# Loading the last 768 columns of one block of output weights as row groups of 63, 54 and 11 partitions

## The chip, the cores and the metric

One core of a Trainium2 chip runs the whole kernel. The metric is the device time of one launch in microseconds (us), as the median of several runs. "Span" is the stretch from the first to the last instruction in one execution that was taken with the hardware profiler. The core has 16 DMA engines, which move data from device memory to the on-chip memory of 128 partitions. The compute engines are PE (matrix), DVE (vector), ACT (scalar) and POOL; SP issues nearly all of the transfers.

## The reference

One token (a row of 1024 numbers) goes through two branches, which a gate mixes:

```python
g = sigmoid((x * gate_w).sum(-1))
a = attention(x)      # 32 query heads, 4 key/value heads, cache of 65536 positions, head size 128
b = mixer(x)          # gelu(x @ w_in), split, layernorm of one half, product, @ w_out
return g * a + (1 - g) * b

# attention
q = x @ wq                                   # 1024 x 4096
p = softmax(q @ k_cache.T * Dh ** -0.5)      # 8 query heads share one key/value head
return (p @ v_cache).reshape(4096) @ wo      # wo: 4096 x 1024
```

All tensors are bf16. The key and value caches are 64 MiB each, `wq` and `wo` 8 MiB each, `w_in` 7 MiB and `w_out` 3.5 MiB: some 162 MB are read once for a result of 2 KB.

## The kernel before, in words

**The stream of loads.** All large inputs pass through one ring in on-chip memory (the region `RING` of the tensor `arena`). The list `stream` fixes their order when the program is built; `load` appends to it and `issue` (L377 to L392) turns entries into transfers on SP's queue. An entry goes out as soon as every ring grain of 1024 columns that it overwrites has been marked as used by `done`. So SP waits for the compute engines and then issues transfers well ahead of the data. Each entry is one transfer of 128 rows, one per partition, and the 16 DMA engines take eight rows each. The order is: `wq`; the keys and values of the four heads in 16 blocks, with `w_in` and `w_out` among the first; then `wo`.

**The output weights.** `rows(A_wo, i, 8)` is quarter i of `wo`: 1024 of its rows, eight to a partition, so one partition receives 8192 numbers (16384 contiguous bytes). Quarters 0, 1 and 2 are one entry each. Quarter 3 is cut by `WO_CUT` into pieces of 5, 2 and 1 of the eight rows, that is 10240, 4096 and 2048 bytes per partition. These six entries end the stream. Just ahead of the very last one `issue` puts a store of the (still zero) output row; the store of the result follows at the end of the program.

**The work on them.** `wo_rows(0)`, `wo_rows(1)`, `wo_piece(2)` and three calls of `wo_piece(3, ...)` multiply the attention output with the six pieces on PE. `spin(n)` puts n matrix products of no use between them. A cast on DVE (L775) and the store (L366) end the kernel.

**Waits.** `Recorder.op` notes each operation with what it reads and writes; `plan` derives the semaphore waits and `emit` writes the instructions. A transfer adds 16 to the semaphore of its ring grain when it is complete, and `op` counts that in `dma_count`; a reader waits for the counted total.

**Small loads.** Four small transfers go out on ACT's queue at the start: `A_x` and `gate_w` as eight rows of 256 bytes each, `B_w_sp` and `B_b_sp` as two bytes each.

Of the kernel before, what the change touches and what calls it, by code (L numbers as in the profile page):

```python
# [17 lines left out]
class Recorder:  # L18
# [9 lines left out]
        self.ahead = 0  # L28
        self.early = 0

    def op(self, eng, fn, r=(), w=(), dma=None):
        o = Op()
        o.eng, o.fn, o.inc, o.count = eng, fn, False, 0
        o.dma = None
        deps = {}
        for k in r:
            if k in self.writer:
                deps[id(self.writer[k])] = (self.writer[k], True)
        for k in w:
            if k in self.writer:  # L40
                deps.setdefault(id(self.writer[k]), (self.writer[k], False))
            for x in self.readers.get(k, ()):
                deps.setdefault(id(x), (x, False))
        o.deps = list(deps.values())
        for k in r:
            self.readers.setdefault(k, []).append(o)
        for k in w:
            self.writer[k] = o
            self.readers[k] = []
        if dma is not None:  # L50
            self.dma_count[dma] = self.dma_count.get(dma, 0) + 16
            o.dma = (dma, self.dma_count[dma])
        o.idx = len(self.ops)
        self.ops.append(o)
        return o
# [40 lines left out]
    def emit(self, nc):  # L96
        waits = self.plan()
        sems = {e: nc.alloc_semaphore("eng_" + e) for e in self.ENGINES}
        dsem = {k: nc.alloc_semaphore("dma_%s" % k) for k in self.dma_count}
        final = {k: v for k, v in self.dma_count.items()}  # L100

        def run(eng, handle):
            for o, ws in zip(self.ops, waits):
                if o.eng != eng:
                    continue
                for d in ws:
                    if d.dma:
                        handle.wait_ge(dsem[d.dma[0]], d.dma[1])
                    else:
                        handle.wait_ge(sems[d.eng], d.count)  # L110
                last = o.fn(handle)
                if o.dma:
                    last.then_inc(dsem[o.dma[0]], 16)
                elif o.inc:
                    last.then_inc(sems[eng], 1)

        body = nc.cur_bb.bb
        gate = next(i for i, x in enumerate(body.instructions)
                    if isinstance(x, mybir.InstDrain) and x.engine == mybir.EngineType.SP)
        first = len(body.instructions)  # L120
        run("SP", nc.sync)
        nc.sync.wait_ge(dsem["out"], final["out"])
        made = list(body.instructions)
        moved = made[first:first + self.ahead]
        assert all(isinstance(x, mybir.InstDMACopy) for x in moved)
        body.instructions = made[:gate] + moved + made[gate:first] + made[first + self.ahead:]
        run("POOL", nc.gpsimd)
        run("PE", nc.tensor)
        first = len(body.instructions)
        run("ACT", nc.scalar)  # L130
        made = list(body.instructions)
        gate = next(i for i, x in enumerate(made) if isinstance(x, mybir.InstDrain) and x.engine == mybir.EngineType.Activation)
        moved = made[first:first + self.early]
        assert all(isinstance(x, mybir.InstDMACopy) for x in moved)
        body.instructions = made[:gate] + moved + made[gate:first] + made[first + self.early:]
        run("DVE", nc.vector)


def bass_gated_mix__gqa_block_cached__mixer_gmlp__decode_kernel(
# [45 lines left out]
    OFF = {}  # L185
# [16 lines left out]
    arena = nc.alloc_sbuf_tensor("arena", [128, NA], BF16)  # L202
# [52 lines left out]
    P = R.op  # L255
# [46 lines left out]
    stream = []  # L302
# [1 line left out]

    GRAN = 1024

    def load(keys, src, off):

        n = len(stream)
        w = src.shape[1]  # L310
        for i, key in enumerate(keys):
            place[key] = (n, off + i * (w // len(keys)), w // len(keys))
        stream.append((keys, off, src))

    def rows(w, i, c):

        return w[128 * c * i:128 * c * (i + 1), :].rearrange("(p c) n -> p (c n)", c=c)
# [12 lines left out]
    def load_k(n, slot):  # L330
        load([("k", n)], kv(A_k_cache, n), slot * SUB)

    def load_k2(n, slot):
        load([("k", n), ("k", n + 1)], kv(A_k_cache, n, True), slot * SUB)

    def load_v2(n, off):
        load([("v", n), ("v", n + 1)], kv(A_v_cache, n, True), off)
# [18 lines left out]
    WO_AT = [0, 8 * DO, 16 * DO, 24 * DO]  # L356
    WO_CUT = [(0, 5), (5, 7), (7, 8)]
    for i in range(3):
        load([("wo", i, 0)], rows(A_wo, i, 8), WO_AT[i])
    for c0, c1 in WO_CUT:  # L360
        load([("wo", 3, c0)], rows(A_wo, 3, 8)[:, DO * c0:DO * c1], WO_AT[3] + DO * c0)

# [2 lines left out]
    def store():  # L365
        P("SP", lambda e: e.dma_start(out[0, 0].rearrange("(q n) -> q n", n=QW), osrc), r=["orow"],  # L366
          w=["out"], dma="out")
# [5 lines left out]
    def grains(off, w):  # L373
        return list(range(off // GRAN, (off + w + GRAN - 1) // GRAN))

    def issue():

        while issued[0] < len(stream):
            n = issued[0]
            keys, off, src = stream[n]  # L380
            w = src.shape[1]
            gr = grains(off, w)
            if any(k not in used for x in gr if x in owner for k in owner[x]):
                return
            for j, x in enumerate(gr):
                owner[x] = (keys[j * len(keys) // len(gr)],)
            if n == len(stream) - 1:
                store()
            P("SP", lambda e, o=OFF["RING"] + off, w=w, src=src: e.dma_start(arena[:, o:o + w], src),
              w=[("slot", x) for x in gr], dma="s%d" % gr[0])  # L390
            issued[0] += 1

    def use(key):
        n, off, w = place[key]
        assert n < issued[0], key
        return arena[:, OFF["RING"] + off:OFF["RING"] + off + w], [("slot", x) for x in grains(off, w)]

    def done(key):
        used.add(key)
        issue()  # L400

    issue()


# [8 lines left out]
      r=["m32"], w=["sel"])  # L413
    P("DVE", lambda e: e.tensor_reduce(mq, vw(idf, 0, [[1, 16], [16, 8]]), AXX, ALU.add), r=["idf"], w=["mq"])
    P("DVE", lambda e: e.tensor_reduce(mhalf, vw(idf, 0, [[32, 2], [64, 2], [1, 32]]), mybir.AxisListType.XY, ALU.add),
      r=["idf"], w=["mhalf"])
# [4 lines left out]
    for fe in range(4):  # L421
        P("POOL", lambda e, fe=fe: e.tensor_copy(vw(sele, 128 * fe, [[32, 4], [1, 32]]),
                                                vw(idb, 64 * (fe // 2) + fe % 2, [[0, 4], [2, 32]])),
          r=["idb"], w=[KSE])
# [5 lines left out]
    def f(e):  # L430
# [7 lines left out]
      r=["oneb", "wsp", "bsp"], w=["mb"])  # L438
# [6 lines left out]
      r=["ones", "gs"], w=[KTB])  # L445
# [4 lines left out]
      r=["g"], w=["omg"])  # L450
# [3 lines left out]
    wqs, keys = use(("wq", 0))  # L454
# [354 lines left out]
```

## Time and profile before

| | |
|---|---|
| median of 9 runs | 381.87 us (381.76 to 382.10) |
| the profiled execution's own time | 381.87 us |
| its span | 380.6 us |
| bytes read | 162.01 MB, 426 GB/s over the span |
| share of the 16 DMA engines' time taken by SP's queue | 98.8% |
| busy: PE, DVE, ACT, POOL | 61%, 54%, 6%, 2% |
| granted clock of PE, mean | 0.848 |

How to read it: the shares of busy time are of the span. The queue named q1 is that of SP, q10 that of ACT; q8 and q14 carry instructions. A "packet" is what one DMA engine moves at a time: here one row of a transfer, or the four bytes with which an engine reports that it is done with its share of one. 1.27 us of the profiled execution's time lie outside the span.

### The profile page before, as it was taken

The page shows a single profiled execution, that of the slowest core. Times are in us where ns is not written, and L with a number is a line of the kernel's source. Part 1 is how long each engine was busy: PE and PEld are TensorE (multiplying, and loading weights), DVE is VectorE, ACT ScalarE, POOL GpSimd, SP SyncE. Part 2 cuts the span into 40 slices and gives each one's busy share as a digit, 9 for nine tenths or more (in the row PEclk, how much of TensorE's full clock was granted, in tenths as well). Part 3 has the DMA queues.
Part 4 walks back from the last instruction along what each step waited for, and adds up shares of the span by engine and source line. Part 5 has one row for each costly group of instructions (what it writes and reads, how often), then busy time and mean ns, then how long its engine had stood idle before and what let it go on. Part 6 is the DMA issues. An engine that isn't in the chain of part 4 may idle for free.

```text
span 380.6 us, 2581 instructions
## 1 busy us (share of the span) xinstructions
PE 232.7 (61%) x1449; PEld 57.8 (15%) x836; DVE 204.4 (54%) x162; ACT 23.2 (6%) x24; POOL 8.4 (2%) x37
## 2 busy tenths in 40 slices
PE   0060488466648924894787328952995983639386
PEld 0010011011101200121111001220111110212024
DVE  4011596678389525965892248745874872412020
ACT  1000000010420000002100000022000000220010
POOL 5000000000000000000000000000000000000000
PEclk9997599798959975999698958985898796959789
DMA  9998989999989999999999999999999999999996
GB/s 441 420 434 372 482 381 443 437 493 424 415 386 441 441 429 434 441 427 413 470 441 441 441 434 427 408 420 441 434 420 425 444 441 441 429 410 437 406 428 251
DMA packets 4254, 162.17 MB, mean 426 GB/s; under 512 B 532, under 2 KB 532, under 8 KB 788
## 3 DMA queue, kind: packets, MB, share of 16 engines
q1 hardware_dynamic: 4208, 162.01, 98.8%
q8 instruction: 9, 0.15, 0.2%
q10 hardware_dynamic: 36, 0.00, 0.0%
q14 instruction: 1, 0.01, 0.0%
HBM read 162.01 MB, written 0.00 MB: 426 GB/s over the span
## 4 chain that ended last, share of the span: by engine, by line
DMA 57%; DVE 21%; PE 20%; ACT 1%; issue 1%; ACTq 0%; SPq 0%; DVEq 0%
DMA arena<-in_A_k_cache_dram 34%; DVE arena L502 17%; DMA arena<-in_A_v_cache_dram 10%; DMA arena<-in_A_wo_dram 8%; PE scp L260 6%; PE scp L262 5%; DMA arena<-in_B_b_sp_dram 5%; PE obt L260 4%; PE obt L262 3%; DVE arena L539 2%; PE fbt L712 1%; ACT arena L534 1%; ACTq L288 0%; PE fbt L660 0%; ACT arena L656 0%
## 5 line engine op out<-in xcount | busy, mean ns | idle before, releaser
L502 DVE STREAM_TRANSPOSE arena<-arena 128x2048 f32<-128x2048 f32 x64 | 142.8, 2282 | 45.8 <-DMA arena<-in_A_k_cache_dram 31.5
L260 PE MATMUL scp<-arena 128*128 128x512 bf16 (+1 forms) x275 | 111.4, 421 | 85.5 <-DVE arena L502 85.0
L262 PE MATMUL scp<-arena 128*128 128x512 bf16 (+1 forms) x279 | 111.0, 416 | 0.0
L260 PE MATMUL obt<-arena 128*64 128x512 bf16 (+2 forms) x334 | 63.1, 418 | 21.0 <-DMA arena<-in_A_v_cache_dram 21.0
L262 PE MATMUL obt<-arena 128*64 128x512 bf16 (+2 forms) x334 | 62.3, 413 | 0.0
L260 PEld LDWEIGHTS scp<-arena 128*128 128x128 bf16 (+1 forms) x275 | 27.4, 103 | 196.2 <-issue 99.9
L539 DVE STREAM_TRANSPOSE arena<-arena 128x2048 bf16<-128x2048 bf16 x7 | 16.2, 2311 | 31.3 <-PE obt L262 29.1
L260 PEld LDWEIGHTS obt<-arena 128*64 128x64 bf16 (+1 forms) x334 | 18.5, 113 | 74.5 <-issue 57.2
L534 ACT ACTIVATE arena<-arena 128x2048 bf16<-128x2048 f32 x8 | 16.0, 2002 | 218.0 <-DVE arena L531 194.9
L519 DVE TENSOR_SCALAR_CACHE_REDUCE arena<-scp 128x2048 f32<-128x2048 f32 x8 | 18.3, 2292 | 16.0 <-PE scp L262 16.0
L580 PE MATMUL mbt<-arena 128*128 128x128 bf16 x16 | 2.0, 264 | 12.6 <-DVE arena L575 12.6
L542 DVE STREAM_TRANSPOSE arena<-arena 128x1024 bf16<-128x1024 bf16 x2 | 2.5, 1245 | 12.5 <-PE obt L262 12.5
L568 DVE RECIPROCAL arena<-mbt 128x1 f32<-128x1 f32 x4 | 0.6, 139 | 15.8 <-PE mbt L563 15.8
L490 POOL COPY arena<-arena 32x32 bf16<-32x32 bf16 x16 | 3.2, 203 | 235.2 <-PE scp L262 211.2
L531 DVE TENSOR_REDUCE arena<-mbt 128x1 f32<-128x32 f32 x4 | 0.8, 191 | 13.8 <-PE mbt L528 13.8
L437 PE MATMUL mbt<-arena 1*128 1x2 bf16 x1 | 0.2, 158 | 12.3 <-DMA arena<-in_B_b_sp_dram 12.3
L439 DVE COPY arena<-mbt 128x2 f32<-128x2 f32 x1 | 0.2, 159 | 12.2 <-PE mbt L437 12.2
L432 PE MATMUL scp<-arena 8*128 8x1 bf16 x8 | 0.6, 196 | 8.7 <-DVE arena L427 8.7
L775 DVE CAST arena<-fbt 36x128 bf16<-36x128 f32 x1 | 0.3, 282 | 10.1 <-PE fbt L712 10.1
L712 PE MATMUL fbt<-arena 128*32 128x128 bf16 x128 | 4.1, 220 | 1.4 <-DMA arena<-in_A_wo_dram 1.4
L712 PEld LDWEIGHTS fbt<-arena 128*32 128x32 bf16 x128 | 3.6, 97 | 3.0 <-DMA arena<-in_A_wo_dram 1.8
L624 ACT ACTIVATE arena<-arena 128x28 f32<-128x28 f32 x1 | 0.2, 227 | 57.8 <-DVE arena L623 57.8
(91 smaller groups left out, 54.8 us busy)
## 6 DMA issues: line engine op xcount, KB each, us to landing
arena<-in_A_k_cache_dram SPq DMA_DIRECT2D x6, 4096.0 KB, 33.2
arena<-in_A_v_cache_dram SPq DMA_DIRECT2D x2, 4096.0 KB, 26.8
arena<-in_B_w_in_dram SPq DMA_DIRECT2D x1, 7168.0 KB, 31.5
arena<-in_A_wo_dram SPq DMA_DIRECT2D x3, 2048.0 KB, 34.2
arena<-in_B_w_out_dram SPq DMA_DIRECT2D x1, 3584.0 KB, 22.1
arena<-in_A_wo_dram SPq DMA_DIRECT2D x1, 1280.0 KB, 31.1
arena<-in_A_wo_dram SPq DMA_DIRECT2D x1, 512.0 KB, 31.8
arena<-in_A_wo_dram SPq DMA_DIRECT2D x1, 256.0 KB, 31.6
```

The source lines that it names most:

```text
L260: return e.matmul(*a, **kw)
L262: one = e.matmul(*a, **kw).ins
L432: ins = e.matmul(tb[:, c:c + 1], vw(xm, c, [[8, 128]], 0, 8), oneb[0:8, 0:1], start=(c == 0), stop=(c == KC - 1), skip_group_check=True)
L490: P("POOL", lambda e, pb=pb: e.tensor_copy(vw(qpad, 24 + 32 * pb, [[QP, 4], [1, 8]], 32 * pb, 32), vw(qall, 8 * g, [[32, 4], [1, 8]], 32 * ...
L502: P("DVE", lambda e: e.transpose(ktb(i).bitcast(F32), sl[:, 4096 * p:4096 * (p + 1)].bitcast(F32)), r=keys[4 * p:4 * p + 4], w=[("kt", i % ...
L519: P("DVE", lambda e: e.tensor_scalar(scs(j), scp[:, :], 0.0, None, op0=ALU.add, op1=ALU.max, accum_out=maxc[:, j:j + 1]), w=[("sc", j % 2) ...
L531: P("DVE", lambda e: e.tensor_reduce(gcol(g, K_NB), mb[:, 0:32], AXX, ALU.min), w=[("nb", g), "mb"])
L534: P("ACT", lambda e: e.activation(psb2, scs(j), ACTF.Exp, bias=gcol(j // 2, K_NB), scale=SCALE, accum_out=lp[:, j:j + 1]), r=[("sc", j % 2 ...
L539: P("DVE", lambda e: e.transpose(ptsb2, psb2), r=["psb"], w=[("ptsb", 0), ("ptsb", 1)])
L542: P("DVE", lambda e: e.transpose(ptsb(n), ab("PSB", 1024, 1024 * (n % 2))), r=["psb"], w=[("ptsb", n % 2)])
L580: ins = e.matmul(mb[:, 0:128], sel[:, 128 * c:128 * (c + 1)], osc[:, 128 * c:128 * (c + 1)], start=(c == 0), stop=(c == 3))
L712: ins = e.matmul(fb[32 * b:32 * (b + 1), 0:QW], ovz[:, z:z + 32], sl[:, o:o + QW], start=False, stop=(i == 3 and c == 7), tile_position=(0 ...
```

## The change

The entry of quarter 0 of `wo` is split into four transfers, which SP issues one after the other. The first carries all 128 partitions without their last 768 columns (14848 of 16384 bytes per partition). The other three carry these 768 columns (1536 bytes per partition) for the partitions 0 to 62, 63 to 116 and 117 to 127. The source of each is viewed as `(i j) n -> i j n` with i = 3, 9 and 11, so that its rows fall to 3, 9 and 11 DMA engines, with 21, 6 and 1 rows for each. All four report to one semaphore, and the count that a reader waits for is 64 in place of 16. The loaded bytes and their places are the same.

```diff
-    def op(self, eng, fn, r=(), w=(), dma=None):
+    def op(self, eng, fn, r=(), w=(), dma=None, parts=1):
...
-            self.dma_count[dma] = self.dma_count.get(dma, 0) + 16
+            self.dma_count[dma] = self.dma_count.get(dma, 0) + 16 * parts
...
                 if o.dma:
-                    last.then_inc(dsem[o.dma[0]], 16)
+                    for x in last if isinstance(last, list) else [last]:
+                        x.then_inc(dsem[o.dma[0]], 16)
...
-    def load(keys, src, off):
+    def load(keys, src, off, cut=None):
...
-        stream.append((keys, off, src))
+        dst = arena[:, OFF["RING"] + off:OFF["RING"] + off + w]
+        parts = [(dst, src)]
+        if cut:
+            c, heights = cut
+            parts = [(dst[:, 0:w - c], src[:, 0:w - c])]
+            p = 0
+            for k, h in heights:
+                parts.append((dst[p:p + h, w - c:w], src[p:p + h, w - c:w].rearrange("(i j) n -> i j n", i=k)))
+                p += h
+            assert p == 128
+        stream.append((keys, off, w, parts))
...
-        load([("wo", i, 0)], rows(A_wo, i, 8), WO_AT[i])
+        load([("wo", i, 0)], rows(A_wo, i, 8), WO_AT[i], cut=(768, ((3, 63), (9, 54), (11, 11))) if i == 0 else None)
...
-            P("SP", lambda e, o=OFF["RING"] + off, w=w, src=src: e.dma_start(arena[:, o:o + w], src),
-              w=[("slot", x) for x in gr], dma="s%d" % gr[0])
+            P("SP", lambda e, todo=todo: [e.dma_start(dst, x) for dst, x in todo],
+              w=[("slot", x) for x in gr], dma="s%d" % gr[0], parts=len(todo))
```

More of the change, by code (lines that the diff above doesn't have):

```diff
@@ L379, in issue @@
             n = issued[0]
-            keys, off, src = stream[n]
-            w = src.shape[1]
+            keys, off, w, todo = stream[n]
             gr = grains(off, w)
```

## The prediction

> **What bounds the kernel now.** I read the page's slices and queues first, then the chain that ended last, then the end of the stream in stretches of 0.2 us, and last the single packets of the trace.
>
> The page, slices and queues:
>
> ```profile
> DMA  9998989999989999999999999999999999999996
> GB/s 441 420 434 372 482 381 443 437 493 424 415 386 441 441 429 434 441 427 413 470 441 441 441 434 427 408 420 441 434 420 425 444 441 441 429 410 437 406 428 251
> q1 hardware_dynamic: 4208, 162.01, 98.8%
> q8 instruction: 9, 0.15, 0.2%
> ```
>
> SP's queue takes 98.8% of all DMA engine time, so the stream of loads is the bound. PE (61%) and DVE (54%) have room. The last slice alone is thin. Nine packets of instructions travel on the same engines.
>
> The chain of waits in its last 36 us (start, length, what):
>
> ```profile
> 345.51 31.10 DMA arena<-in_A_wo_dram
> 376.60 0.14 issue
> 376.74 1.75 PE fbt L712 x56
> 378.49 0.01 issue
> 378.50 0.42 PE fbt L712 x8
> ```
>
> PE waits for the first piece of quarter 3 until 376.60, multiplies two pieces (1.75 us), and at 378.50 starts on the third; in the timeline PE's weight loads idle 0.19 us for that third transfer. So data and PE arrive together, and both follow the stream's end.
>
> The end of the stream, windows (the last two columns are the DMA share and GB/s):
>
> ```profile
> 375.80:376.00 0.20, 0.20 (x3) 0.00 (x0) 0.00 (x0) 0.00 (x0) 0.00 (x0) 1.00 0.91 358
> 376.40:376.60 0.20, 0.00 (x0) 0.00 (x0) 0.00 (x0) 0.00 (x0) 0.00 (x0) 1.00 0.54 216
> 377.40:377.60 0.20, 0.20 (x16) 0.20 (x11) 0.00 (x0) 0.00 (x0) 0.00 (x0) 1.00 0.53 205
> 377.60:377.80 0.20, 0.20 (x15) 0.20 (x10) 0.00 (x0) 0.00 (x0) 0.00 (x0) 1.00 0.20 72
> ```
>
> A share of 0.54 is 9 of 16 engines: seven have finished by 376.4, nine go on for over a microsecond, and few are left after 377.6. The engines do not end together, and a load lands when its slowest engine is done. This is what the change acts on.
>
> **Which engines are late.** The trace gives no engine number, but the packets can be threaded. On one engine a packet starts 3 or 4 ns before the one ahead ends, and each engine takes eight rows of a load and then four bytes. That gives 16 chains. Eight of them also carry the 256-byte rows of `A_x`, `gate_w` and the early store; these are transfers of eight rows, so I call these engines the lower half. The two-byte loads of one row run on one of these eight: the first engine. Ends of the chains (us):
>
> ```
> lower: 375.949 376.113 376.150 376.177(first) 376.299 377.085 377.751 377.978
> upper: 376.007 376.424 377.576 377.600 377.612 377.694 377.734 377.983
> ```
>
> Each chain that ends after 377.5 met one instruction packet, which took 0.98 to 1.11 us and delayed the packet behind it by about half as much again, in all some 1.5 us. The lower chain at 377.085 met an 8192-byte instruction packet at 87.7 us and fell back 0.95 us. The first engine met none.
>
> The packets came to the halves in the order upper, lower, lower, upper five times, and the last one at 377.98 fell to the engine of the first again. That is a rotation over eight engines. If they are neighbours, and the first engine is not among them, they are the seventh to fourteenth, and the two late lower ones are the seventh and eighth. That is inferred, not shown.
>
> **The change part by part.**
>
> *Bytes per engine.* Packet starts lie 80 ns apart for 2048 bytes and 612 ns for 16384, so 0.0371 ns per byte and 61 ns for a row of 1536. The shorter main transfer saves each engine 8 x 1536 x 0.0371 = 0.456 us. The row groups give engines 1 to 3 21+6+1 = 28 rows, engines 4 to 9 seven, engines 10 and 11 one, the others none, with 6 ns for each report:
>
> - engines 1 to 3: 28 x 0.061 + 0.018 - 0.456 = +1.27 us
> - engines 4 to 9: 7 x 0.061 + 0.012 - 0.456 = -0.02 us
> - engines 10 and 11: 0.061 + 0.006 - 0.456 = -0.39 us
> - engines 12 to 16: -0.456 us
>
> *What it makes of the end.* The first engine goes from 376.18 to 377.45, and two other early ones to at most 376.30 + 1.27 = 377.57; both are below the present end. The upper late ones gain at most 0.46. But the lower engine at 377.978 is in no row group's favour: as one of engines 4 to 8 it ends at 377.978 - 0.017 = 377.96, against 377.983 for the latest before. The sum is -0.02 us. If the engine at 377.085 is the second or third, it ends at 378.355, and the sum is +0.37. All gains of the upper half are thrown away, since the load still waits for that lower engine.
>
> *Issues.* Three more transfers on SP. The six issues of `wo` took 328 to 1610 ns, so 1.0 to 4.8 us. They are issued at 329.5; the loads of quarters 0 and 1 go out together and SP then has nothing to issue until 345.13. The second quarter's issue slips to 336.4 at most; its first packet is due at 361.1. Cost 0, with 24 us of cover.
>
> *The wait for quarter 0.* The issue was at 329.5 and the landing took 34.2 us (page, median of the three), so about 363.7; PE takes it at 365.56, after the last softmax sum. Engines 1 to 3 may be late on it by 1.27 us: 364.97. Cost 0, cover 0.6 us. The later loads carry the shift on to the end, which is what is summed above.
>
> *PE.* Its products are the same. PE idles 0.49 us ahead of 376.74, so it could follow the stream by up to that.
>
> *Rows in other partitions.* Before, each engine of a 128-row load writes eight partitions of its own; now the row groups come in consecutive runs of 21, 6 and 1, so that they enter partitions that other engines are writing. The trace has few such packets: the 256-byte rows of `A_x` on eight engines took 18 ns, beside full streams, and nothing around them stretched. The other end is the first packets of the run, 2.716 to 3.568 us for the 2.418 of undisturbed ones of 65536 bytes, up to 1.48 times. I take zero, from rows of the same kind of transfer; with 1.48, engines 1 to 3 need another 28 x 0.061 x 0.48 = 0.82 us: 378.39, +0.41. If a row took twice as long, as when two share one way in (an estimate), 377.57 + 1.71 = 379.28, +1.30.
>
> [...]
>
> Total: 381.87 (profiled execution and median alike) - 0.02 = **381.85 us**.
>
> **The rivals.**
>
> *A late lower engine is the second or third (slower).* Then 377.978 or 377.751 grows by 1.27, to 379.25 or 379.02: +1.27 or +1.04, 382.9 to 383.15. It decides as soon as an engine that ends after 376.7 stands among the first three. For it: the trace does not number them, and two drawn at random from the seven other lower ones hit one of these two in 11 of 21 cases. Against it: the order of the instruction packets, which fits neighbours only at seven and eight. 0.20.
>
> *Rows in foreign partitions cost.* +0.41 to +1.30 as above, 382.3 to 383.2. For it: 28 small rows behind one another on three engines. 0.12, of which 0.07 over the bound below.
>
> *The lower engine is not the limit in the timed runs (gain).* If there only engines 12 to 16 are late, the end follows them: at most -0.456, 381.4. Against it: 377.978 beside 377.983 in the profiled execution, whose time is the median itself. 0.05, with 0.02 for more than that by something that I do not see.
>
> *It does not do what it says.* Were all 128 rows on one engine: 376.18 + 128 x 0.061 - 0.456 = 383.5, +5.5 us, 387.4. The transfers of eight rows and of one row do spread as said. 0.03.
>
> **How the numbers follow.** Unchanged, with +0.37 included: 0.60. About 0.2% (0.76 us) is what a measurement of this kernel can tell from no change. Within it: 0.60, 0.05 of the foreign partitions, 0.03 of the gain: 0.68. Slower: 0.20 + 0.07 + 0.03 = 0.30. Faster: 0.02. The likeliest case alone spans 381.7 to 382.3. The range of 381.4 to 383.2 takes in the full gain and a late engine among the first three; outside are the one-engine case and what exceeds the bounds, under 0.1.
>
> **What would show it.** Right: 128 packets of 1536 bytes; the stream's last packet at 377.9 to 378.0 again; a DMA share from 376.4 to 377.4 above the old 0.54, since three early engines work on to about 377.5; PE's third piece near 378.5. Wrong: last packets after 378.7 with one to three engines at work alone (late engine in front), packets of 1536 bytes well over 65 ns (foreign partitions), or PE's wait for quarter 0 going beyond 365.6.

## The result and the profile after

The kernel is slower: 383.16 us (median of 9 runs, 382.77 to 383.84) against 381.85 us (median of 29). The ratio is 1.0038, with a 95% interval of 1.003 to 1.0046: **+1.31 us**. The time lies inside the predicted range, but the likeliest case, no change, is wrong. The profiled execution of the changed kernel took 383.16 us as well, with a span of 381.8 us.

The page of the changed kernel, slices and packets:

```profile
DMA  9999989999999999999999999999999999999995
GB/s 440 433 439 419 412 386 436 439 492 433 427 439 419 405 414 439 439 426 439 434 433 439 439 439 433 434 439 439 433 391 424 457 426 439 441 412 422 386 410 241
DMA packets 4411, 162.17 MB, mean 425 GB/s; under 512 B 561, under 2 KB 689, under 8 KB 945
q1 hardware_dynamic: 4365, 162.01, 98.8%
q8 instruction: 9, 0.15, 0.2%
```

The engines are as busy as before, with the same bytes. SP's queue has 4365 packets where it had 4208: 157 more. 128 of them are the new rows of 1536 bytes, so 29 are reports. The change as described would bring 3 + 9 + 11 = 23; 29 is 9 + 9 + 11. **By this count the group of 63 rows ran on nine engines with seven rows each, not on three with 21.** That puts 7 + 6 + 1 = 14 rows on each of engines 1 to 9, and one on engines 10 and 11. The view `(i j) n -> i j n` does not change the addresses. Why 63 rows went to nine engines was not shown. In the experiment on the last piece below, groups of 57, 64 and 7 rows without any view brought 26 reports (4218 packets, 10 more than before, with 16 reports for that piece before), which is 3 + 16 + 7.

The chain of waits at its end (start, length, what):

```profile
345.62 32.20 DMA arena<-in_A_wo_dram
377.82 0.14 issue
377.95 2.17 PE fbt L722 x64
380.13 0.03 issue
```

The same chain, with the landing of quarter 3's first piece at 377.82 in place of 376.60: 1.22 us later. Everything behind it moved along.

Windows of 0.2 us at the end of the stream (last columns: granted clock, DMA share, GB/s):

```profile
376.40:376.60 0.20, 0.20 (x12) 0.13 (x6) 0.00 (x0) 0.00 (x0) 0.00 (x0) 1.00 0.92 369
377.40:377.60 0.20, 0.06 (x1) 0.00 (x0) 0.00 (x0) 0.00 (x0) 0.00 (x0) 1.00 0.85 338
378.00:378.20 0.20, 0.20 (x10) 0.20 (x12) 0.00 (x0) 0.00 (x0) 0.00 (x0) 1.00 0.58 225
378.80:379.00 0.20, 0.20 (x15) 0.20 (x10) 0.00 (x0) 0.00 (x0) 0.00 (x0) 1.00 0.08 31
```

By 376.4 six engines had finished before, and a seventh did at 376.42; now the first one ends at 377.09. So it is not only one group that became late: all engines did. Threaded again (packets followed along each engine as in the prediction), the early chains end at 377.09 to 377.73 (before 375.95 to 376.42), the late upper ones at 378.13 to 378.36 (before 377.58 to 377.98), the one behind the 8192-byte instruction packet at 378.59 (before 377.09), and the last two at 378.960 and 379.195, both of the lower half and both behind an instruction packet. Threading is less sure here than before, since packets that slow each other do not follow at a fixed distance.

Where the time was lost, in the 4 us in which the new rows move; the first line is the kernel before, the second the changed one:

```profile
360.00:364.00 4.00, 4.00 (x21) 1.05 (x10) 0.00 (x0) 0.00 (x0) 0.00 (x0) 0.50 0.99 422
```

```profile
360.00:364.00 4.00, 4.00 (x22) 1.01 (x10) 0.00 (x0) 0.00 (x0) 0.00 (x0) 0.50 1.07 340
```

The share stays at about one while the rate falls from 422 to 340 GB/s: packets last longer. The packet records say which ones (rows that start between 355 and 369.5 us):

```
row size     before, ns (median / highest)     after, ns (median / highest)
1536         -                                 83 / 189
14848        -                                 559 / 1002
16384        615 / 626                         618 / 1116
```

An undisturbed row of 1536 bytes takes 65 ns (the least of the 128 here, and 65 to 67 in the run with one tail transfer). The rows of the main transfer of quarter 0 and of quarter 1 are slowed too. Against the undisturbed duration of each size, the packets from 355 to 369.5 us took 17.2 us longer in all, 17.2 / 16 = 1.08 us for each engine; in the kernel before the same sum is zero, give or take a few tenths of a microsecond by the choice of the undisturbed duration. Only some 3 us of it are in the short rows themselves.

### The profile page after: what moved, and what is told of

The parts are those of the page before. It is cut to its first block, busy times and chain, and to the rows that moved or that the text cites. A ratio compares the mean times of both kernels' runs of the same rounds, so it can differ in the third digit from the quotient of the medians.

```text
span 381.8 us, 2584 instructions
## 1 busy us (share of the span) xinstructions
PE 232.6 (61%) x1449; PEld 57.8 (15%) x836; DVE 204.5 (54%) x162; ACT 23.2 (6%) x24; POOL 9.4 (2%) x37
## 3 DMA queue, kind: packets, MB, share of 16 engines
q1 hardware_dynamic: 4365, 162.01, 98.8%
## 4 chain that ended last, share of the span: by engine, by line
DMA 64%; DVE 17%; PE 17%; issue 1%; ACTq 0%; SPq 0%; DVEq 0%
DMA arena<-in_A_k_cache_dram 41%; DVE arena L512 15%; DMA arena<-in_A_v_cache_dram 9%; DMA arena<-in_A_wo_dram 8%; DMA arena<-in_B_b_sp_dram 5%; PE scp L261 5%; PE scp L263 4%; PE obt L261 3%; PE obt L263 3%; DVE arena L549 1%; PE fbt L722 1%; ACTq L289 0%; DVE arena L585 0%; DVE arena L583 0%; SPq L399 0%
## 5 line engine op out<-in xcount | busy, mean ns | idle before, releaser
L261 PE MATMUL obt<-arena 128*64 128x512 bf16 (+2 forms) x334 | 63.9, 423 | 19.6 <-DMA arena<-in_A_v_cache_dram 19.6
L263 PE MATMUL obt<-arena 128*64 128x512 bf16 (+2 forms) x334 | 63.2, 419 | 0.0
L447 PE MATMUL mbt<-arena 1*128 1x2 bf16 x1 | 0.2, 158 | 12.4 <-DMA arena<-in_B_b_sp_dram 12.4
L449 DVE COPY arena<-mbt 128x2 f32<-128x2 f32 x1 | 0.2, 159 | 12.4 <-PE mbt L447 12.4
```

Of the source, the lines that this page charges most:

```text
L261: return e.matmul(*a, **kw)
L263: one = e.matmul(*a, **kw).ins
```

## The experiments

Each is an edit of the changed kernel. The expectations weigh three theories: B, that only the bytes on each engine count; P, that rows cost in partitions which other engines write ("foreign" ones; the trace records no partitions, so "own" and "foreign" are the author's reading, and the times of the rows are what is measured); S, that short rows or more transfers cost by themselves. "Excess" is the sum just described. The kernel before, timed beside them, took 381.81 us for one tail transfer, the two halves and the tails of 16 rows, 381.84 for the last piece, and 381.78 for the others.

**One tail transfer.**

```diff
-cut=(768, ((3, 63), (9, 54), (11, 11)))
+cut=(768, ((16, 128),))
```

> The last 768 columns of quarter 0 go as one transfer of 128 rows, eight per DMA engine, each engine in the partitions that it also writes in the main transfer. No bytes move between engines. Theory P (two engines that write the same group of partitions slow each other): rows of 1536 bytes take 65 ns, 8 x 0.061 + 0.006 - 0.456 = +0.04 us. Theory S (short rows, or one more transfer in the queue, cost time by themselves): a good part of the 0.9 us that the bytes do not explain, +0.5 to +0.9 us. Theory B (only the bytes on each engine count): +0.04 us.

Measured: 381.94 us, ratio 1.0003 (0.9994 to 1.0012). The same window:

```profile
360.00:364.00 4.00, 4.00 (x21) 1.06 (x10) 0.00 (x0) 0.00 (x0) 0.00 (x0) 0.50 1.02 423
```

The rows of 1536 bytes took 65 to 67 ns, and the excess is 0.37 us. Short rows and one more transfer cost nothing that can be told. For many more transfers theory S is still open here.

**Two halves of the partitions.** Full rows, two transfers of 64 partitions:

```diff
-            c, heights = cut
-            parts = [(dst[:, 0:w - c], src[:, 0:w - c])]
...
+            parts = [(dst[x:x + cut], src[x:x + cut]) for x in range(0, 128, cut)]   # cut = 64
```

> Quarter 0 goes as two transfers of 64 partitions with full rows of 16384 bytes, four rows per engine in each. Bytes per engine as before, no short rows, one more transfer; but both halves of the engines write the same 64 partitions at a time. Theory P: rows of 16384 bytes take up to twice the 611 ns, up to 8 x 0.61 = +4.9 us, less where the engines are out of step (2 us apart at the end): +2 to +4.9 us. Theories S and B: no more than +0.1 us.

Measured: 388.5 us, ratio 1.0182 (1.0168 to 1.0196), +6.7 us.

```profile
360.00:364.00 4.00, 3.39 (x17) 1.00 (x10) 0.00 (x0) 0.00 (x0) 0.00 (x0) 0.50 1.02 225
```

With the rows of 64 neighbouring partitions spread over all 16 engines (SP's queue has 4224 packets, 16 reports more than before) the rate is 225 GB/s, about half of 422, at a full DMA share. Of the 169 rows of 16384 bytes that start between 355 and 369.5 us 168 were slowed, to 1194 ns in the median, against 615 before. That is P, and it costs more than its upper end of 4.9: the excess of 98 us is 6.1 us for each engine, and 8 us of it are in rows of 32768 bytes, which belong to the load ahead.

**Even and odd partitions.** The same but for the partitions:

```diff
+            parts = [(dst[x:128:cut], src[x:128:cut]) for x in range(cut)]   # cut = 2
```

> Quarter 0 goes as two transfers of 64 full rows, the even and the odd partitions, four rows per engine in each: the same packets on the same engines as with the lower and the upper half of the partitions, which cost 6.7 us. Theory P with ways in that are shared by groups of partitions spread over all 128: each transfer now reaches all of them, so clearly less than 6.7 us, 1 to 4 us. If it is only that an engine leaves its own partitions (theory F), or the 64-row shape or the reading side (theory S): 6.7 us again.

Measured: 381.77 us, ratio 0.9999 (0.999 to 1.0008), no row of 16384 bytes over 625 ns between 355 and 369.5 us.

```profile
360.00:364.00 4.00, 4.00 (x24) 1.04 (x12) 0.00 (x0) 0.00 (x0) 0.00 (x0) 0.57 1.02 434
```

Neither the 64-row shape nor the reading of rows in another order costs; which partitions are written at a time decides. The loss is below the 1 to 4 us expected of P, namely none. Which partitions of a 64-row transfer each engine takes was not measured. So it stays open whether each engine kept to its usual ones here, or whether sharing costs nothing when it is spread over all 128.

**Tails of 16 rows, 8 partitions apart, and consecutive.**

```diff
+            for x in range(heights):                                              # heights = 8
+                parts.append((dst[x:128:heights, w - c:w], src[x:128:heights, w - c:w]))
```
```diff
+cut=(768, ((16, 16),) * 8)
```

> The last 768 columns of quarter 0 go as eight transfers of 16 rows, partitions 8 apart, one row per engine in each. Bytes per engine as before. Theory P: mostly two engines at one group of partitions; 8 x 0.067 - 0.456 = +0.08 us without meeting, up to +0.6 us when each row takes twice as long. Theory S: more than with one tail transfer, +0.5 us or above. Theory B: +0.08 us.

> As the one before, with the same packets on the same engines in the same order, but each transfer of 16 rows covers 16 consecutive partitions, so that four engines write one group of four. Theory P: rows take up to four times as long, 0.08 + 8 x 3 x 0.061 = up to +1.5 us, and more than with partitions 8 apart. Theories S and B: the same as with partitions 8 apart.

Measured: 382.92 us, ratio 1.0032 (1.0019 to 1.0044), and 382.76 us, ratio 1.0029 (1.0017 to 1.004). No bytes move between engines, and yet about 1 us is lost; excess 11.7 and 10.6 us. First the one, then the other:

```profile
360.00:364.00 4.00, 4.00 (x24) 1.09 (x12) 0.00 (x0) 0.00 (x0) 0.00 (x0) 0.55 1.05 358
```

```profile
360.00:364.00 4.00, 4.00 (x22) 1.05 (x10) 0.00 (x0) 0.00 (x0) 0.00 (x0) 0.50 1.02 353
```

B falls. But P's detail was wrong as well: the first was to cost 0.6 us at most and cost 1.1, and consecutive partitions were to be worse, and are not. S, with +0.5 us or more for eight more transfers and the same for both, forecast this pair better; what rules it out is the run with extra rows in own partitions below, where seven more transfers add no more than their bytes. Most of the excess (10.5 of 11.7 us, and 9.6 of 10.6) is in the long rows, little in the short ones. So a short row would meet another engine's long rows more than other short rows. With engines up to 2 us out of step that fits, but it is argued.

**Three engines in truth.** The first group has 57 rows, three times 19, and a fourth takes the six that are left:

```diff
-cut=(768, ((3, 63), (9, 54), (11, 11)))
+cut=(768, ((3, 57), (9, 54), (11, 11), (6, 6)))
```

> The row groups are 57, 54, 11 and 6, so that the first really falls to three engines (19 rows each): engines 1 to 3 get 27 rows, 4 to 6 eight, 7 to 9 seven, 10 and 11 one, the others none. This is the spread that the change describes. By bytes alone (theory B, the nine-engine split is the cause of the loss): engines 1 to 3 go from 376.3 to 377.5, the lower late ones keep their end, 381.85. Theory P (rows in other engines' partitions cost): as with the change, +0.9 to +1.4 us, with rows of 1536 bytes well over 65 ns, since as many rows lie in other engines' partitions.

Measured: 382.67 us, ratio 1.0023 (1.0014 to 1.0033), +0.89 us. SP's queue has 4365 packets, so 29 reports more than before, which is 3 + 9 + 11 + 6. Excess 17.3 us, as with the change; rows of 1536 bytes took 96 ns in the median.

```profile
360.00:364.00 4.00, 4.00 (x30) 1.00 (x12) 0.00 (x0) 0.00 (x0) 0.00 (x0) 0.70 1.04 321
```

P again, at its lower end, where B had +0.07. The threading, now with the classes of engines told apart by their rows (engines 1 to 3, 4 to 6, 7 and 8, 9, 10 and 11, 12 to 16), puts no instruction packet ahead of the end on engines 1 to 3: one late lower engine is among 4 to 6, one is the seventh or eighth. The first three end at 378.21, 378.53 and 378.68, and the latest engine, of 12 to 16, at 378.70. So here the first three were the right ones to load, and the rows ate more than the spread could give. By its bytes alone an engine that ends at 377.75 or later before would have ended here at 377.75 + 27 x 0.061 + 0.018 - 0.456 = 378.96 or later, and none does (an estimate, from the prediction's own terms).

**The same extra rows in own and in foreign partitions.** Quarter 0 whole, and 56 more rows to columns that nothing else uses by then (the issue also waits until they are free). The first run's partitions are those taken as own; the second run's are 64 higher:

```diff
+            spare = ab("KT", 768, 6144)
+            for x in (0, 1, 2, 3, 32, 33, 34):
+                x += cut                              # 0, or 64
+                parts.append((spare[x:x + 29:4, :], src[x:x + 29:4, w - 768:w]))
```

> Quarter 0 loads as before, and ahead of the next entry seven transfers of eight rows of 1536 bytes go to unused columns: 56 rows more, seven on each engine of the lower half. [...] Only the bytes per engine change: 7 x 0.067 = +0.47 us on engines 1 to 8. All theories: +0.4 to +0.5 us if a lower engine is the last at the end, 0 to +0.3 us if an upper one is; rows of 65 ns.

> As the one before, with the same packets on the same engines, but the partitions are 64 higher, where the engines of the upper half write. Theories S and B: the same time as with the own partitions. Theory P: rows of 1536 bytes over 65 ns and the upper engines' rows slowed; more by 0.3 to 0.8 us than with the own partitions.

Measured: 382.34 us, ratio 1.0015 (1.0006 to 1.0023), +0.56 us; and 382.97 us, ratio 1.0035 (1.0023 to 1.0048), +1.19 us. In own partitions, then in foreign ones:

```profile
360.00:364.00 4.00, 4.00 (x22) 0.96 (x10) 0.00 (x0) 0.00 (x0) 0.00 (x0) 0.51 1.00 411
```

```profile
360.00:364.00 4.00, 4.00 (x22) 1.06 (x10) 0.00 (x0) 0.00 (x0) 0.00 (x0) 0.50 1.01 345
```

In own partitions the rows took 65 to 67 ns (excess 1.2 us), and the bytes cost the +0.47 of the sum or little more: a lower engine is last. In foreign ones the same packets, by their shape on the same engines (4320 on SP's queue in both runs, 56 rows and 56 reports more than before), cost 0.63 us on top (excess 12.4 us, 11.9 of it in rows of 16384 bytes). The slowest run in own partitions, 382.53, lies below the fastest in foreign ones, 382.83. This is the cleanest pair for P. Threaded at the end, it also shows who pays. The six late upper chains end at 377.57 to 377.73 with the rows in own partitions, and at 378.30 to 378.65 with the rows in foreign ones, so the upper engines lose, which agrees with the reading that they write there. But the engines that carry the rows lose as well: the five early lower chains end at 377.17 to 377.45 in place of 376.60 to 376.79.

**The aim at the last piece.** With the bytes set by the ends in the traces:

```diff
+        load([("wo", 3, c0)], ..., cut=(57, 64, 7) if c0 == 7 else None)
...
+            p, parts = 0, []
+            for h in cut:
+                parts.append((dst[p:p + h], src[p:p + h]))
+                p += h
```

> Quarter 0 loads as before. The last piece of quarter 3 (128 rows of 2048 bytes, 80 ns apart) goes as groups of 57, 64 and 7 rows, on 3, 16 and 7 engines with 19, 4 and 1 rows each: engines 1 to 3 get 24 rows, 4 to 7 five, the others four, in place of eight. It is the aim of the change at the end of the stream, with bytes chosen for the ends that the traces show. Theory B (bytes alone): the first three end at 376.3 + 1.3 = 377.6, the late lower ones at 377.98 - 0.24 = 377.74, 0.24 us faster, 381.6. Theory P (rows in other engines' partitions cost 0.10 to 0.14 us of DMA engine time each, over 16 engines 0.8 to 1.1 us for some 120 rows): slower by 0.4 to 0.9 us, 382.2 to 382.7.

Measured: 382.58 us, ratio 1.0017 (1.0008 to 1.0026), +0.74 us. From 374 to 378 us, before and here:

```profile
374.00:378.00 4.00, 3.50 (x103) 2.70 (x97) 0.00 (x0) 0.00 (x0) 0.00 (x0) 1.00 0.74 296
```

```profile
374.00:378.00 4.00, 3.40 (x103) 2.76 (x98) 0.00 (x0) 0.00 (x0) 0.00 (x0) 1.00 0.84 296
```

The engines are busier (0.84 against 0.74) and move no more (296 GB/s). The rows of 2048 bytes took 101 ns in the median, where they took 84 before. The rows of 4096 bytes just ahead took up to 288, where none had taken over 172. So the engines are slowed while they share the work, and the last row ends at 378.24 in place of 377.98. P's forecast of 0.4 to 0.9 holds. None of the nine beats the kernel before.

## Why the prediction was wrong

**What held.** The bound, the chain, and PE's and DVE's cover: SP's three further issues, the wait for quarter 0 (its first product ran at 365.65, where it had been 365.56) and PE's products cost nothing that shows. The row's own time held, 61 ns apart: seven rows for each lower engine in own partitions gave +0.56 for the +0.47 worked out.

**First step that failed: "engines 1 to 3: 28 rows".** The groups gave engines 1 to 9 fourteen rows each. By the prediction's own terms that is 14 x 0.061 + 0.018 - 0.456 = +0.42 us on the late lower engines, in place of -0.02, whichever of the eight lower engines they are. The rival that the change does not do what it says was named, but with one engine as its case, not nine. The 29 added reports show the nine, where the change as described would have brought 23.

**Second step that failed: "Rows in other partitions ... I take zero".** It is the larger part. The kernel with three engines in truth, where the late lower engines get no more bytes than they lose, stands at +0.89; the changed kernel's +1.31 is 0.42 above it, as much as the byte term. So the sum that the runs support is some 0.4 for the bytes and some 0.9 for the meeting of rows. The split is an estimate: the intervals of the two kernels overlap. The threaded ends agree with it, since the last lower chain moved from 377.978 to 379.195, by 1.22 us, of which 0.42 are bytes and 0.80 are left. The row chosen as nearest, 256 bytes in 18 ns, was a bad witness: the rows of 1536 bytes hold only some 3 of the 17.2 us themselves, and the rest falls on long rows. The prediction had the mechanism as a rival at 0.12, and its price of 0.41 to 1.30 covers the measured 0.9. That is in part luck, since the price counted only the short rows of engines 1 to 3, while all engines were slowed, by 1.08 us each.

**The doubled price.** That the prediction's +1.30 for rows of twice the length stands beside the measured +1.31 is luck: it was worked out from 28 rows of doubled length on three engines, and there were 14, of 83 ns in the median. The doubling of short rows was the author's estimate; in the kernel with three engines in truth the median was 96 ns. Long rows did double in the two halves of 64 partitions: 1194 ns against 615, at 225 GB/s in the window shown. With the even and odd partitions none took over 625, at 434 GB/s. The rival deserved more than its 0.12.

**The late lower engine in front.** The rival with the highest chance gave +1.04 to +1.27, and the time of +1.31 would have looked like its proof. It is not: with 14 rows each, no engine of the changed kernel had the 28 rows that this rival needs, and where three engines did get 27, in the run with 57 rows, they were early ones. The inference that the late lower ones are the seventh and eighth found no support: in that run one of them is among the fourth to sixth. Since the instruction packets fall differently from kernel to kernel, that does not settle it for the kernel before.

**What would be left to gain.** In the trace of the kernel before, each chain that ends after 377 us carried an instruction packet (0.98 to 1.11 us each on the eight that end after 377.5). What they still have to move is their eight rows of each load, and rows in foreign partitions slow engines at that, as the pair of own and foreign partitions shows (+0.56 and +1.19 us). The experiment on the last piece is one such trade, at a loss. A split of the work that gives those engines fewer bytes and enters no foreign partitions was not tried.

## What to carry to other kernels

A DMA engine is not a free hand: in these runs 56 rows cost 0.56 us in own partitions and 1.19 us in foreign ones, where long rows were slowed as well (11.9 us of the excess of 12.4), so balancing engines by moving rows can lose more than the imbalance. When packets lengthen while the DMA share stays at one, look at which partitions are written at the same time, and compare the same packets on own and on foreign partitions. And count the reports to see on how many engines a transfer really ran, since the view here was meant for 3, 9 and 11 engines, 23 reports, and brought 29.

## What the runs showed of the hardware that was not expected

- Rows in foreign partitions cost DMA engine time: 10.6 to 17.3 us in the kernels with 128 of these short rows, 0.08 to 0.14 us for each, and 12.4 - 1.2 = 11.2 us for 56 rows in the other half, 0.20 us each. That is more than the 61 ns of the row itself.
- A load split into halves of 64 neighbouring partitions ran at 225 GB/s, one split into 64 even and 64 odd ones at 434 GB/s (from 360 to 364 us).
- With three more transfers SP's last issue of `wo` was held: 0.35 us before, and in the changed kernel

```profile
347.00 6.00 SPq L399 DMA_DIRECT2D arena<-in_A_wo_dram  x1
```

It cost nothing, since its data were due only some 23 us after it. Every kernel with two or more added transfers had an issue near the end that took 2.4 to 7.2 us, and none with one; why was not tested.
- By the threading, which engine an instruction packet hits differs from kernel to kernel: in the kernel before, the halves were hit in the order upper, lower, lower, upper five times; in the changed one upper six times, then lower twice. Eight engines, two of them in the lower half, in both.
